# Routing products copied out of PSUM before they are scaled: one fused attention and mixture-of-adapters kernel on one core

## The chip, the cores and the metric

The kernel runs on one core of one Trainium2 chip. A core has five engines that work side by side, each through its own list of instructions in order: TensorE (PE) for matrix products, VectorE (DVE), ScalarE (ACT) and GpSimd (POOL) for elementwise work, and SyncE (SP), which here only issues transfers. Matrix products land in PSUM, eight banks of 512 fp32 columns on 128 partitions; everything else works in SBUF. The metric is the device time of one execution in microseconds; the time before is 117.84 us, the median of three runs (117.83 to 118.19).

## The reference

Linear attention with cosine weights, and then a mixture of low-rank adapters on its output. Eight batches, eight heads, 576 positions, 64 numbers a head; eight adapters of rank 16, of which each token uses two. The last lines are given in words.

```python
def phi(x, c, s):
    r = np.maximum(x, 0.0)
    return np.concatenate([r * c, r * s], axis=-1)
q_p = phi(q, cos_w, sin_w)
k_p = phi(k, cos_w, sin_w)
kv = np.einsum('bhsf,bhsd->bhfd', k_p, v)
z = np.sum(k_p, axis=2)
num = np.einsum('bhsf,bhfd->bhsd', q_p, kv)
den = np.einsum('bhsf,bhf->bhs', q_p, z)[..., None] + 1e-06
x = num / den                      # as (4608, 512)
...
logits = x @ w_gate                # 8 adapters, the best two are kept
w = softmax over the two
out = x + sum over the two of w[e] * (x @ A[e]) @ B[e]
```

Inputs are 28.85 MB of fp32 (q, k, v of 9.44 MB each and the weights), the output 9.44 MB.

## The kernel before

The work is cut into small named steps, and their order is written out by hand in one string, ORDER. A token of it such as `nd26@2` or `ex24=V` names a step, after `=` the engine that does it (V is DVE, S is ACT, G is POOL), and after `@` the buffer slots that it takes, most often PSUM banks 0 to 7. `replay` walks through the string and emits step by step; each engine gets its instructions in this order, and the framework adds the waits that the data and the buffers need. Nothing is decided on the chip: an engine whose next step isn't ready waits, and what is queued behind it waits too.

The steps, in the order in which the data goes through them:

- `LK`, `LQ`, `LV`: loads of a batch (or of two: K4, K6, Q4 and Q6 hold batches 4 and 5, or 6 and 7). All go through SP's queue. A load may only be issued when the slot that it fills is free: V7 takes V4's slot (`V_AT`), Q6 the slots of Q0 and Q3.
- `cK`, `cQ`: conversion of a third of a load to bf16; `phiK`, `phiQ`: multiplication of one of nine slices by the tangent; `vs`: multiplication of one of nine slices of V by the cosine (`vs4` does V4 and V5, `vs6` V6 and V7).
- `kv`: products of K and V on PE, `ke`: their copy out of PSUM.
- `tq`: transpose of a tile of Q on PE, `eq`: its copy out of PSUM. There are 36 tiles of 128 tokens; tiles 18 to 26 belong to batches 4 and 5, tiles 27 to 35 to batches 6 and 7.
- `nd`: numerator and denominator on PE; `rd`: reciprocal of the denominator, `nx`: the division, both DVE. `nx26` stands for tiles 26 and 27.
- `tx`, `ex`: transpose of the quotient and its copy.
- `za`: the product with the adapters A and the gate, 136 columns a tile, for a group of up to three tiles in one bank. A group is named by its last tile: 20, 23, 26, 29, 32, then 34 (two tiles) and 35 (one).
- the routing of a group, small steps all: `mx` (the two best), `nt` (their sum), `ge` (which adapters are kept), `d`, `sg` (a sigmoid on ACT), `w` (the weights), `zg` (the 128 adapter columns of each tile times the weights). `ge`, `d` and `zg` read the products from the bank that `za` wrote, which is free only after `zg`.
- `tz`, `ez`: transpose of the scaled products and its copy; `dx`: the quotient plus the product with B on PE, 512 columns; `eo`: the copy to an output buffer; `st`: the store of a group.

`fill` steps are products that nobody reads; they keep PE busy early on. The steps around the last loads stand so in ORDER before:

```
vs4.0=G@1,2 ... vs4.6=G ... LV7@1 ... st8.0 ...
st11.0 tq25 phiQ6.1=G ex20=S@1 mx19 dx15@2 vs6.0=S@0,1 vs6.8=V vs6.4=G dx16 tq26@0 eq24=V@1
...
tz20@7 phiQ6.6=G zg23 ke6=S@1 tq30@0 tz23@6 ... nd26@2 ... nx26@6 dx19 tq31 eo18=S@5 eq30=V@0 nd28@2
```

and at the end

```
za35@4 eo30=S@4 w34=G dx32@6 mx35@1 zg34 nt35=V tz34@7 eo32=S ge35 ez34=V@2 d35 dx33@2 st32.0
sg35 dx34 w35=G zg35 eo33=S@2 tz35@0 ez35=V@0 dx35@6 st34.0 eo35=S@0 st35.0
```

The functions that the change touches:

Of the kernel before, what the change touches and what calls it, by code (L numbers as in the profile page):

```python
# [18 lines left out]
NJ = 9  # L19
# [79 lines left out]
w11=G phiQ4.2=G cQ4.2=S@2 kv5.1 phiQ4.4=V kv5.2 phiQ4.1=V mx14 tx16@2 phiQ4.5=V nt14=G tq18@4
zg11 ke5=S@0 phiQ4.8=G tx17 tq19 ge14 d14 ex16=S@0 phiQ4.3=V za15@6 eq18=V@0 sg14 za16 w14=G  # L100
za17 cK6.1=S@2 tz11@3 mx15@0 tq20@4 mx16 mx17 ez11=V@2 tq21 ge17 nd18@0 cK6.2=V@0 eq20=S@1
phiK6.3=G zg14 nd19 phiK6.8=G nt17=V d17 tz14@7 rd18@2 sg17 tq22@4 phiK6.5=G ez14=S@0 nx18@1
tq23 cK6.0=S@4 phiQ4.6=G dx11@7 w17=V dx9@2 eq22=V@0 dx10 phiK6.0=G tx18@0 eo9=S@3 tx19
phiK6.4=V dx12@4 phiK6.7=G ex18=V@0 dx13 eo11=S cQ6.0=G@4 zg17 nd20@0 eo12=S@4 nd21 tz17@6
rd20@0 za18@7 nx20@0 ez17=S@1 tq24@4 phiQ6.2=G phiK6.2=S dx14@6 cQ6.1=G@0 phiQ4.7=S nd22@0
eo14=V nd23 mx18@0 tx20@6 st14.0 rd22@0 phiQ6.0=G tx21 phiQ6.3=S nx22@4 za19 st11.0 tq25
phiQ6.1=G ex20=S@1 mx19 dx15@2 vs6.0=S@0,1 vs6.8=V vs6.4=G dx16 tq26@0 eq24=V@1 eo15=S@5 tq27
vs6.5=G dx17@6 eq26=V@0 vs6.7=G nd24@2 eo17=S nd25 vs6.6=G phiK6.1=S za20 st17.0 rd24@0 tx22@6
mx20 tq28@0 vs6.2=G vs6.1=S nx24@3 st5.0 tq29 nt20=G vs6.3=S tx23 st2.0 cQ6.2=G@2 d20 kv6.0@2
ge20 sg20 ex22=V@0 phiQ6.4=S kv7.0@4 w20=V za21@6 phiK6.6=G eq28=S@1 zg20 za22 za23 mx21@1  # L110
kv7.1 mx22 mx23 ge23 kv7.2 nt23=G d23 kv6.1 ke7=V@3 sg23 kv6.2 w23=G tz20@7 phiQ6.6=G zg23
ke6=S@1 tq30@0 tz23@6 phiQ6.5=G ez20=S@2 nd26@2 ez23=V@0 nd27 phiQ6.8=V phiQ6.7=G dx18@6 rd26@0
nx26@6 dx19 tq31 eo18=S@5 eq30=V@0 nd28@2 nd29 dx21@6 rd28@2 nx28@5 tx24@0 dx22 tx25 eo21=S@2
tx26@1 tx27 ex24=V@0 nd30@2 nd31 dx20@0 rd30@1 nx30@2 tq32@6 eo20=S tq33 ex26=S@1 dx23@0
eq32=V@1 za24@3 tx28@2 za25 eo23=S tx29 za26 mx24@2 ex28=S@0 nd32@4 st23.0 mx25 mx26 ge26 nd33
nt26=V st20.0 d26 tq34@1 rd32@2 sg26 nx32@7 za27@0 w26=G eq34=S@0 tx30@2 za28 tx31 za29 mx27@1
tx32@5 ex30=S@0 mx28 tx33 mx29 zg26 nd34@6 nt29=G ge29 ex32=S@1 tz26@4 rd34@0 tq35@1 d29 nx34@0
za30@3 za31 sg29 ez26=V@0 za32 eq35=S@0 w29=G tx34@5 mx30@2 dx24@6 zg29 dx25 ex34=S@0 mx31 mx32
tz29@4 nt32=V nd35@0 ge32 eo24=S@2 d32 ez29=V@1 dx26@5 rd35@0 za33@2 nx35@1 sg32 dx27@6 eo26=S
w32=G dx28 zg32 st26.0 za34 eo27=S@1 mx33@0 tz32@4 mx34 dx29@3 ez32=V@2 nt34=G tx35@5 d34  # L120
dx30@0 eo29=V ex35=S@0 dx31 ge34 sg34 st29.0 za35@4 eo30=S@4 w34=G dx32@6 mx35@1 zg34 nt35=V
tz34@7 eo32=S ge35 ez34=V@2 d35 dx33@2 st32.0 sg35 dx34 w35=G zg35 eo33=S@2 tz35@0 ez35=V@0
dx35@6 st34.0 eo35=S@0 st35.0
# [67 lines left out]
def a_ps(n):  # L191
    return 0.16 + n / 1200.0
# [14 lines left out]
def kernel(  # L207
# [68 lines left out]
    W0, L0 = {}, {}  # L276
# [17 lines left out]
    R_zt, R_o, R_rd, R_sm = Res("zt", NZT), Res("o", NO + 3), Res("rd", 3), Res("sm", 3)  # L294
    R_ps = Res("ps", 8)
# [51 lines left out]
    o_half = add("half", {"DVE": 0.1}, [], e_half, alloc=[al(L0, "o", R_o, 3, cnt=3, only=NO)])  # L347
# [37 lines left out]
    def load(dst, src, bs):  # L385
        ap = src[bs[0]:bs[0] + len(bs)].rearrange(
            "b (g hp) (p j) d -> (hp p) (b g) (j d)", hp=2, j=NJ)
        nc.sync.dma_start(out=dst, in_=ap)  # L388
# [9 lines left out]
    for l in LOADS:  # L398
        nm, b = l[0], int(l[1])
        G = {}  # L400
        if nm == "V":
            lds[l] = (G, add("L" + l, {"SP": 0.7}, [],
                             lambda e, G=G, b=b: load(v_t[:, H2 * G["s"].slot:H2 * (G["s"].slot + 1)], v, [b]),
                             alloc=[al(G, "s", R_v, NJ, only=V_AT[b])], dma=BYT))
        else:
            units, tl, src, res = (K_UNITS, k_t, k, R_k) if nm == "K" else (Q_UNITS, q_t, q, R_q)
            bs = next(us for us in units if us[0] == b)
            nb = len(bs)
            lds[l] = (G, add("L" + l, {"SP": 0.7}, [],
                             lambda e, G=G, bs=bs, nb=nb, tl=tl, src=src:  # L410
                             load(half(tl, G["s"].slot, nb), src, bs),
                             alloc=[al(G, "s", res, 3, cnt=nb, align=nb,
                                       only=K_AT[b] if nm == "K" else None)],
                             dma=BYT * nb))
# [4 lines left out]
    def add_phi(nm, u, bs):  # L419
# [4 lines left out]
        G, ld = lds[nm + str(b)]  # L424
        for c in range(3):
# [277 lines left out]
    for bt in split(EX_TAIL):  # L703
# [22 lines left out]
        for ti in bt:  # L726
            X[ti]["ex"] = ex

    for ids in groups:
        n = len(ids)  # L730
        Gd = {}
        zas, mxs = [], []
# [167 lines left out]
```

## Time and profile before

| | |
|---|---|
| median of three runs | 117.84 us (117.83 to 118.19) |
| profiled execution, its own time | 118.06 us |
| span of its instructions | 116.3 us |
| mean granted TensorE clock | 0.976 |
| busy: PE, DVE, ACT, POOL | 98.2, 86.1, 84.1, 62.6 us |
| read and written by transfers | 28.85 and 9.44 MB |

The page of the profile gives the busy time of each engine, then the span in 40 equal slices, one digit a slice (9 is 90% or more). The chain of waits starts from the last instruction and goes back to what released each step. In a group's row stand line, engine, operation, tiles written and read, and shapes; then the count, the total busy time and the mean of one in nanoseconds, and the idle time of the engine just before. In a row of the timeline the first number is the start, the second the length, both in microseconds. "issue" is time in which an engine waited for nothing that the profile shows.

### The profile page before, as it was taken

The numbers are of one execution on the slowest core, as the hardware profiler recorded it, in microseconds if no ns is written. First come the engines' busy times: TensorE is split into PE (matmuls) and PEld (weight loads), VectorE is DVE, ScalarE is ACT, GpSimd is POOL, SyncE is SP. The second block draws the span as 40 slices with busy tenths as digits, with TensorE's granted clock in tenths as the row PEclk, the third lists the DMA queues.
The fourth block names the chain that finished last, engine by engine and source line by source line (L and its number), as shares of the span: only waits on it lengthen the run. The fifth ranks groups of instructions, "written<-read, shape, count | busy, mean of one in ns | idle before, by whom it ended". The sixth has DMA issues, their size and how long they took to land.

```text
span 116.3 us, 4552 instructions
## 1 busy us (share of the span) xinstructions
PE 98.2 (84%) x1954; PEld 73.5 (63%) x1954; DVE 86.1 (74%) x211; ACT 84.1 (72%) x126; POOL 62.6 (54%) x119
## 2 busy tenths in 40 slices
PE   5999988679595959999987869999999699999830
PEld 1344465469494948686866766785897588976200
DVE  1157766394789989999899888797998788887510
ACT  7305568394998887997959798987993349897850
POOL 3074678259169699649978346995967000101100
PEclk9999999985999999999999999999999999999996
DMA  2999999999999999999999999999996001923994
GB/s 42 388 401 391 393 391 392 393 305 390 392 392 387 392 391 393 387 391 392 392 394 385 393 391 391 388 413 406 386 406 264 23 0 46 414 92 129 378 403 172
DMA packets 15827, 38.57 MB, mean 332 GB/s; under 512 B 1728, under 2 KB 1728, under 8 KB 15808
## 3 DMA queue, kind: packets, MB, share of 16 engines
q1 hardware_dynamic: 15808, 38.29, 87.8%
q8 instruction: 15, 0.25, 0.9%
q14 instruction: 4, 0.03, 0.1%
HBM read 28.85 MB, written 9.44 MB: 329 GB/s over the span
## 4 chain that ended last, share of the span: by engine, by line
PE 36%; DMA 29%; DVE 14%; ACT 8%; SPq 4%; issue 4%; POOL 1%; POOLq 0%; DVEq 0%; ACTq 0%
DMA q<-in_q_dram 14%; DMA v<-in_v_dram 14%; PE psum L604 8%; DVE x L692 6%; PE psum L837 6%; PE psum L738 5%; PE psum L713 5%; SPq L388 4%; PE psum L654 4%; PE psum L500 4%; DVE qt L623 3%; ACT o L302 2%; PE psum L647 2%; ACT qt L621 2%; PE psum L799 1%
## 5 line engine op out<-in xcount | busy, mean ns | idle before, releaser
L604 PE MATMUL psum<-ident,qp 128*128 128x128 bf16 x288 | 21.5, 226 | 1.9 <-DVE qp L313 1.8
L692 DVE TENSOR_TENSOR x<-psum,rd 128x1024 bf16<-128x1024 f32 (+1 forms) x19 | 22.2, 1168 | 1.1 <-PE psum L864 0.6
L313 POOL TENSOR_SCALAR kp<-kp,tanw 128x256 bf16<-128x256 bf16 (+1 forms) x29 | 16.7, 587 | 10.0 <-ACT kp L440 10.0
L604 PEld LDWEIGHTS <-qp 128*128 128x128 bf16 x288 | 18.2, 102 | 3.1 <-DVE qp L313 1.9
L313 POOL TENSOR_SCALAR vb<-v,cosw 128x256 bf16<-128x256 f32 (+1 forms) x30 | 17.6, 604 | 3.1 <-DMA v<-in_v_dram 3.1
L440 ACT ACTIVATE kp<-k 128x768 bf16<-128x768 f32 (+1 forms) x12 | 12.5, 1054 | 7.5 <-DMA k<-in_k_dram 7.1
L864 PE MATMUL psum<-ident 128*128 128x512 bf16 (+1 forms) x70 | 16.4, 388 | 1.4 <-POOL ident masks.py:199 1.4
L623 DVE TENSOR_SCALAR qt<-psum 128x2048 bf16<-128x2048 bf16 x12 | 14.5, 1219 | 1.3 <-PE psum L604 1.2
L713 PE MATMUL psum<-ident,x 128*128 128x128 bf16 x144 | 12.5, 221 | 3.0 <-DVE x L692 2.8
L304 POOL CAST qp<-q 128x768 bf16<-128x768 f32 (+1 forms) x10 | 11.2, 1128 | 6.3 <-DMA q<-in_q_dram 6.3
L302 ACT COPY o<-psum 128x1024 f32<-128x1024 f32 (+1 forms) x12 | 9.9, 840 | 6.4 <-PE psum L837 6.2
L837 PE MATMUL psum<-x,ident 128*64 128x512 bf16 (+1 forms) x48 | 13.9, 385 | 0.6 <-DVE x L692 0.6
L837 PE MATMUL psum<-Bb,zt 128*64 128x512 bf16 (+1 forms) x48 | 13.8, 379 | 0.3 <-DVE zt L306 0.2
L713 PEld LDWEIGHTS <-x 128*128 128x128 bf16 x144 | 9.8, 114 | 6.1 <-DVE x L692 2.5
L738 PE MATMUL psum<-AW,xt 128*128 128x136 bf16 x144 | 12.7, 223 | 0.9 <-ACT xt L302 0.4
L621 ACT ACTIVATE qt<-psum 128x2048 bf16<-128x2048 bf16 (+1 forms) x7 | 11.4, 1628 | 2.2 <-PE psum L604 2.1
L313 POOL TENSOR_SCALAR qp<-qp,tanw 128x256 bf16<-128x256 bf16 (+1 forms) x20 | 11.5, 583 | 2.7 <-DVE qp L306 2.5
L500 PE MATMUL psum<-vb,kp 64*128 64x65 bf16 x576 | 11.7, 190 | 1.4 <-issue 0.6
L864 PEld LDWEIGHTS <-ident 128*128 128x128 bf16 x70 | 7.0, 104 | 9.1 <-issue 2.4
L780 POOL TENSOR_TENSOR w<-ge,ex 128x24 f32<-128x24 f32 (+2 forms) x10 | 2.3, 231 | 18.8 <-ACT ex L776 18.7
L500 PEld LDWEIGHTS <-kp 64*128 64x128 bf16 x576 | 9.9, 94 | 3.2 <-issue 1.5
L654 PE MATMUL psum<-kv,qt 128*64 128x65 bf16 x384 | 9.8, 197 | 2.1 <-issue 1.6
(60 smaller groups left out, 172.7 us busy)
## 6 DMA issues: line engine op xcount, KB each, us to landing
v<-in_v_dram SPq DMA_DIRECT2D x8, 1152.0 KB, 16.0
q<-in_q_dram SPq DMA_DIRECT2D x4, 1152.0 KB, 15.0
k<-in_k_dram SPq DMA_DIRECT2D x4, 1152.0 KB, 10.0
k<-in_k_dram SPq DMA_DIRECT2D x2, 2304.0 KB, 19.9
q<-in_q_dram SPq DMA_DIRECT2D x2, 2304.0 KB, 19.8
out_dram<-o SPq DMA_DIRECT2D x6, 768.0 KB, 5.5
out_dram<-k SPq DMA_DIRECT2D x5, 768.0 KB, 5.7
out_dram<-o SPq DMA_DIRECT2D x1, 512.0 KB, 2.7
```

Of the source, the lines that this page charges most:

```text
L313: eng.tensor_scalar(out=o_ap, in0=i_ap, scalar1=by, scalar2=0.0, op0=ALU.mult, op1=ALU.add)
L440: nc.scalar.activation(o_ap, i_ap, AF.Relu)
L500: nc.tensor.matmul(out=psum[:, s + hp, h2 * W:(h2 + 1) * W], lhsT=kp[hp * 64:hp * 64 + 64, bi * H2 + h2, :], rhs=vb_t[hp * 64:hp * 64 + 64 ...
L604: nc.tensor.transpose(out=o_ap[:, h2, :, hi, :], in_=qv[:, bi * H2 + h2, :], identity=ident)
L621: nc.scalar.activation(o_ap, i_ap, AF.Relu)
L623: nc.vector.tensor_scalar(out=o_ap, in0=i_ap, scalar1=0.0, scalar2=None, op0=ALU.max)
L654: nc.tensor.matmul(out=psum[hi * 64:hi * 64 + 64, s + g, x * W:(x + 1) * W], lhsT=qt[:, qi, h2, hp, hi, :], rhs=kv_t[KV[b]["kv"].slot][:, ...
L692: nc.vector.tensor_tensor(out=x_t[Y["x"].slot][:, 0:n].rearrange("p n (g i d) -> p (n g) i d", g=2, i=4), in0=f()[:, :, :, 0:D], in1=r().t ...
L713: nc.tensor.transpose(out=bank16(s, 1024)[:, i * 512 + c * 128:i * 512 + (c + 1) * 128], in_=xv[:, c, :], identity=ident)
L738: nc.tensor.matmul(out=psum[:, s, i * ZW:(i + 1) * ZW], lhsT=xt_t[Z["xt"].slot][:, zi, c, :], rhs=AW[:, c, :], start=(c == 0 and i == 0), ...
L837: nc.tensor.matmul(out=o, lhsT=w, rhs=r, start=not last, stop=bool(last), skip_group_check=True)
L864: nc.tensor.matmul(out=psum[:, s % 8, c:], lhsT=ident, rhs=warm[:, c:], start=s < 8, stop=True, skip_group_check=True)
```

## The change

Three things are changed. First, for the groups 18-20, 21-23, 24-26, 27-29 and 30-32 (`ZS_GROUPS`), which hold the tiles of batches 4 to 7 but for the last three, a new step `zc` copies the products of `za` (408 fp32 columns) from PSUM to an SBUF buffer `zs`; the bank is free when `zc` and the three `mx` are done. `ge`, `d` and `zg` then read the copy, and `zg` may run on POOL. The buffers `zs` lie in `k_t[1]`, the tile that K6 is the last to fill, and can be used once K6 is converted. Second, of the last four stores the two that hold three tiles are split into one of two tiles and one of one tile (`ST_SPLIT`); each part waits only for its own copy. Third, ORDER is another: all five `zc` are on ACT, `zg20`, `zg26` and `zg29` on POOL, `zg23` and `zg32` on DVE; the last loads come as V7, V6, Q6 instead of Q6, V6, V7; and the groups 34 and 35 are routed side by side.

```diff
+ST_SPLIT = 4
+ZS_GROUPS = (6, 7, 8, 9, 10)
...
+    ZS_LAST, NZS = 5, 4
+    zs_t = [k_t[1].rearrange("p g x -> p (g x)")[:, 3 * ZW * i:3 * ZW * (i + 1)].rearrange(
+        "p (n z) -> p n z", z=ZW) for i in range(NZS)]
...
-                     alloc=[al(Gd, "za", R_ps, 1)] if i == 0 else [],
+                     alloc=[al(Gd, "za", R_ps, 1 + n * zcopy)] if i == 0 else [],
...
+            if zcopy:
+                return zs_t[Gd["zs"].slot][:, 0:n]
             return psum[:, Gd["za"].slot, 0:n * ZW].rearrange("p (n z) -> p n z", z=ZW)
...
+            def e_zc(e, Gd=Gd, n=n):
+                copy(e, zs_t[Gd["zs"].slot][:, 0:n].rearrange("p n z -> p (n z)"),
+                     psum[:, Gd["za"].slot, 0:n * ZW])
+            zcs = [add(f"zc{ids[-1]}", {"ACT": a_ps(n * ZW), "DVE": d_ps32(n * ZW)}, zas[-1:], e_zc,
+                       alloc=[al(Gd, "zs", R_zs, 1)], free=[(Gd, "za")])]
...
-            nc.vector.tensor_tensor(
+            eng = nc.vector if e == "DVE" else nc.gpsimd
+            eng.tensor_tensor(
                 out=sm("zg"),
...
-        o_ge = add(f"ge{ids[-1]}", {"DVE": 0.175}, [mxs[-1]], e_ge)
-        o_d = add(f"d{ids[-1]}", {"DVE": 0.18}, [o_nt], e_d)
+        o_ge = add(f"ge{ids[-1]}", {"DVE": 0.175}, [mxs[-1]] + zcs, e_ge)
+        o_d = add(f"d{ids[-1]}", {"DVE": 0.18}, [o_nt] + zcs, e_d)
...
+        cuts = [(0, 2), (2, 3)] if n == 3 and gi >= len(outs) - ST_SPLIT else [(0, n)]
+        for y, (i0, i1) in enumerate(cuts):
+            def e_st(e, i0=i0, i1=i1, rows=rows, Gd=Gd):
+                nc.sync.dma_start(out=rows[:, i0:i1], in_=o_t[Gd["o"].slot][:, i0:i1, :])
```

The loading code is rewritten so that a load could be cut in parts, but each load stays one transfer. Of the new ORDER, the places that the prediction speaks of:

```
vs4.0=G@1,2 ... vs4.2=S ... vs4.7=G vs4.1=S ... vs4.4=G ... vs4.6=G vs4.8=S ... vs4.3=G vs4.5=S ... LV7@1 ... LV6@0 ... LQ6@2 ... st8.0
...
zc20=S@0 eq24=V@1 tx23 dx15@6 cQ6.2=S@0 cQ6.0=G@4 za21@4 dx16 mx20 mx21@1 nd24@0 ex22=V@0 nd25
eo15=S@4 phiQ6.2=G ge20 dx17@5 phiQ6.1=V vs6.3=G za22 rd24@0 eo17=S tq26@6 nx24@2 za23 phiQ6.0=G
vs6.4=S st17.0 st2.0 zc23=S@1 vs6.5=V tq28@0 phiK6.4=S nt20=V kv7.0@2 mx22 mx23 ge23 tq27 nt23=G
d23 d20 tq29 sg23 vs6.7=V sg20 w23=G kv7.1 eq26=V@0 eq28=S@1 w20=G kv7.2 zg20=G kv6.0@4 kv6.1
zg23=V cQ6.1=G@2 kv6.2 ke7=V@2 tz23@6 ke6=S@0 tz20@7 ez23=V@2 nd26@0 ez20=S@1 phiQ6.8=V nd27
phiQ6.5=G phiQ6.3=S dx21@4 rd26@2 phiQ6.4=G nx26@5 dx22 tq30@6 eo21=S@5 tq31 dx18@0 eq30=V@0
phiQ6.6=S dx19 nd28@2
...
zc26=S@2 ... eq35=S@0 ... zc29=S@0 ... ex32=S@1 ... zc32=S@3 ... ex35=S@0
...
za35@2 eo27=S@3 za34 mx35@1 tz32@7 dx29@6 nt35=V ez32=V@2 d35 eo29=S dx30@0 st29.0 mx34 ge35 dx31
nt34=V sg35 d34 st29.1 ge34 dx32@4 sg34 w35=V eo30=S@5 w34=G zg35 zg34 tz35@2 ez35=V@1 tz34@5
eo32=S dx35@6 st32.0 ez34=V@0 dx33@0 st32.1 eo35=V@1 dx34 st35.0 eo33=S@4 st34.0
```

More of the change, by code (lines that the diff above doesn't have):

```diff
@@ L103 @@
[L103 to L114, printed above, removed]
@@ new lines @@
+tq26@6 nx24@2 za23 phiQ6.0=G vs6.4=S st17.0 st2.0 zc23=S@1 vs6.5=V tq28@0 phiK6.4=S nt20=V
+kv7.0@2 mx22 mx23 ge23 tq27 nt23=G d23 d20 tq29 sg23 vs6.7=V sg20 w23=G kv7.1 eq26=V@0 eq28=S@1
+w20=G kv7.2 zg20=G kv6.0@4 kv6.1 zg23=V cQ6.1=G@2 kv6.2 ke7=V@2 tz23@6 ke6=S@0 tz20@7 ez23=V@2
+nd26@0 ez20=S@1 phiQ6.8=V nd27 phiQ6.5=G phiQ6.3=S dx21@4 rd26@2 phiQ6.4=G nx26@5 dx22 tq30@6
+eo21=S@5 tq31 dx18@0 eq30=V@0 phiQ6.6=S dx19 nd28@2 eo18=S@2 nd29 tq32@6 rd28@2 nx28@6 tx24@0
+tx25 tq33 tx26@1 eq32=S@1 tx27 ex24=V@1 nd30@2 nd31 ex26=V@0 dx20@0 rd30@2 za24@1 nx30@7 za25
@@ L124 @@
+zg32=V za35@2 eo27=S@3 za34 mx35@1 tz32@7 dx29@6 nt35=V ez32=V@2 d35 eo29=S dx30@0 st29.0 mx34
+ge35 dx31 nt34=V sg35 d34 st29.1 ge34 dx32@4 sg34 w35=V eo30=S@5 w34=G zg35 zg34 tz35@2
+ez35=V@1 tz34@5 eo32=S dx35@6 st32.0 ez34=V@0 dx33@0 st32.1 eo35=V@1 dx34 st35.0 eo33=S@4
+st34.0
 """
@@ L727 @@
             X[ti]["ex"] = ex
-    for ids in groups:
+    for gi, ids in enumerate(groups):
         n = len(ids)
```

156 lines of the change are left out of this document (87 added, 69 removed).

## The prediction

> **What bounds the kernel now.** I read the slices of the page first, then the busy time by stage, the chain of waits in order of time, and last the timeline at the places the chain named.
>
> ```profile
> DMA  2999999999999999999999999999996001923994
> GB/s 42 388 401 391 393 391 392 393 305 390 392 392 387 392 391 393 387 391 392 392 394 385 393 391 391 388 413 406 386 406 264 23 0 46 414 92 129 378 403 172
> ```
>
> A slice is 116.3 / 40 = 2.91 us. The transfers run at about 390 GB/s without a gap until slice 30, fall to nothing near 93 us, and come back for the stores. So there are two stages: up to about 80 us the loads set the pace, and after that something else does.
>
> ```profile
> 70.00:80.00 10.00, 9.66 (x179) 7.03 (x173) 8.03 (x15) 8.16 (x13) 7.60 (x10) 1.00 1.04 399
> 80.00:90.00 10.00, 9.79 (x303) 8.40 (x302) 9.23 (x22) 7.66 (x12) 8.33 (x13) 1.00 0.90 363
> 90.00:100.00 10.00, 8.97 (x210) 7.62 (x208) 8.49 (x16) 5.81 (x8) 0.24 (x1) 1.00 0.17 66
> 100.00:110.00 10.00, 9.60 (x129) 6.36 (x127) 7.79 (x33) 8.83 (x14) 1.09 (x5) 1.00 0.57 230
> 110.00:116.30 6.30, 1.55 (x6) 0.31 (x4) 0.52 (x2) 1.81 (x3) 0.21 (x1) 0.83 0.75 297
> ```
>
> The columns after the stage's length are PE, PE's weight loads, DVE, ACT and POOL, then granted clock, DMA share and GB/s. From 80 to 110 us PE and DVE are both nearly full, ACT has room except in the last ten, POOL does almost nothing after 90, and the clock is full. The chain shows which of them hands on:
>
> ```profile
> 63.30 16.49 DMA v<-in_v_dram
> ...
> 87.74 0.45 PE psum L604 x8
> ...
> 89.63 1.24 DVE x L692
> ...
> 90.90 0.32 PE psum L654 x8
> 91.22 0.62 issue
> ...
> 105.49 0.86 PE psum L837 x4
> ...
> 106.63 0.26 DVE m L749 x2
> ...
> 111.42 0.40 PE psum L837
> 111.85 0.59 ACT o L302
> ```
>
> The last load, V7, lands at 63.30 + 16.49 = 79.79. One DVE result (nx26) holds the chain until 90.86, PE carries it to 106.6, then comes the routing of the last two groups, and the last copy ends at 111.85 + 0.59 = 112.44. What follows to 116.3, 3.86 us, is the last store and the end of the program.
>
> ```profile
> 79.88 0.73 ACT L310 ACTIVATE vb<-v,cosw 128x512 bf16<-128x512 f32 x1 [0.72 <-DMA v<-in_v_dram]
> 79.89 0.49 DVE L313 TENSOR_SCALAR vb<-v,cosw 128x512 bf16<-128x512 f32 x1 [0.78 <-DMA v<-in_v_dram]
> 79.95 0.99 POOL L313 TENSOR_SCALAR vb<-v,cosw 128x512 bf16<-128x512 f32 x1 [1.23 <-DMA v<-in_v_dram]
> ```
>
> Three engines stood idle for 0.7 to 1.2 us until that load came: there is no backlog at 79.9 us. The kernel is therefore 79.9 us of loading, about which the change can do little, and 36.4 us of tail, where everything has to be won or lost.
>
> **The change, part by part.** *The loads.* The same bytes are loaded; the last three become V7, V6, Q6 in place of Q6, V6, V7. V7 goes into V4's slot, so its issue must wait for the nine vs4 steps, and V6 and Q6 now queue behind that wait on SP. In the kernel before:
>
> ```profile
> 55.05 4.07 POOL L313 TENSOR_SCALAR vb<-v,cosw 128x512 bf16<-128x512 f32 x6 [0.28 <-DMA v<-in_v_dram]
> 57.41 8.65 SPq L388 DMA_DIRECT2D v<-in_v_dram  x2
> ```
>
> V4 and V5 are in by 55.05. The new order gives five vs4 steps to POOL (5 x 0.68 = 3.4) and four to ACT, so V7 can be issued at about 59. What is already queued then (up to K6) lasts until the three last loads have their turn: 4.72 MB at 0.392 MB/us is 12.0 us, 79.8 - 12.0 = 67.8. Less the 2 or 3 us of a transfer's way, there are about 6 us of cover. I cost this at nothing; without cover each us of lateness would be a us of the result. The rearranged work up to 80 us likewise hides behind the transfers, which the slices show saturated. So the last load again lands at 79.9.
>
> *From the load to tile 28's products (nd28).* The rows for this part:
>
> ```profile
> L623 DVE TENSOR_SCALAR qt<-psum 128x2048 bf16<-128x2048 bf16 x12 | 14.5, 1219 | 1.3 <-PE psum L604 1.2
> L783 DVE TENSOR_TENSOR zg<-psum,w 128x384 bf16<-128x384 f32 x11 | 6.0, 549 | 0.1
> L313 DVE TENSOR_SCALAR qp<-qp,tanw 128x512 bf16<-128x512 bf16 x5 | 2.1, 440 | 0.0
> L313 DVE TENSOR_SCALAR vb<-v,cosw 128x512 bf16<-128x512 f32 x2 | 1.0, 479 | 0.8 <-DMA v<-in_v_dram 0.8
> L304 POOL CAST qp<-q 128x1536 bf16<-128x1536 f32 x4 | 5.9, 1463 | 0.3 <-DMA q<-in_q_dram 0.3
> L313 POOL TENSOR_SCALAR qp<-qp,tanw 128x512 bf16<-128x512 bf16 x9 | 6.2, 695 | 0.2
> L780 POOL TENSOR_TENSOR w<-ge,ex 128x24 f32<-128x24 f32 x8 | 1.9, 236 | 15.9 <-ACT ex L776 15.8
> L780 POOL TENSOR_TENSOR w<-ge,ex 128x8 f32<-128x8 f32 x1 | 0.2, 206 | 1.8 <-ACT ex L776 1.8
> L776 ACT ACTIVATE ex<-d 128x24 f32<-128x24 f32 x11 | 2.4, 222 | 0.4 <-DVE d L766 0.3
> 84.77 0.48 DVE L780 TENSOR_TENSOR w<-ge,ex 128x24 f32<-128x24 f32 x1
> 86.77 0.70 DVE L306 CAST kv<-psum 128x520 bf16<-128x520 f32 x1
> 90.77 1.22 DVE L623 TENSOR_SCALAR qt<-psum 128x2048 bf16<-128x2048 bf16 x1
> ```
>
> On DVE, before, 79.89 to 90.86 is 10.97 us from the load to the end of nx26. In the new order this stretch loses eq24 (1.22, now ahead of the load), vs6.8 (0.48), w20 (0.48) and zg20 (0.55), the last two to POOL; it gains phiQ6.1 (0.44), vs6.5 and vs6.7 (0.96) and nt20 (estimated at 0.2, from POOL's small forms): -2.73 + 1.60 = -1.1. phiQ6.1 must wait for POOL's cast cQ6.0, 1.46 after the load, where DVE would come to it at 1.2: +0.3. So nx26 ends at 90.86 - 0.8 = 90.1, and eq30, which began at 90.77, can begin at 90.1.
>
> eq30 also needs tq31, and that hangs on POOL, since Q6 now lands last: cQ6.0, phiQ6.2, vs6.3, phiQ6.0, then nt23, w23, w20 and **zg20**, then cQ6.1, phiQ6.5, phiQ6.4. w20 can't start before d20 on DVE and two sg steps on ACT (2 x 0.22). Behind d20 come vs6.7 and eq26 (0.48 + 1.22) and the steps from ke7 to nx26, 90.86 - 86.77 = 4.1 before, with 0.5 of idle in it: 90.1 - 1.7 - 3.6 = 84.8 at the latest, so w20 starts at 85.3. Until there POOL's first four steps (1.46 + 3 x 0.7 = 3.6, to 83.5) have 1.8 us to spare. From there it goes step by step: 0.24 + zg20 + 1.46 + 2 x 0.695, and 0.45 for tq31. No row has zg on POOL. From below: a one-input step of 512 elements takes 0.695, so some 0.6 for 384. From the same operation: 206 ns for 8 elements and 236 for 24 are 1.9 ns an element, 0.206 + 376 x 0.0019 = 0.92. From above: twice that, 1.8, if DVE gets in its way (the two w's quoted show what a collision does: DVE's took 480 ns beside a busy POOL). I take 0.92, the nearest row; tq31 then ends at 89.8, just in time.
>
> [...]
>
> *The second thing the copy does* is turn ge, d and zg of groups 20 to 32 into DVE operations that read both operands from SBUF, where they read one from PSUM.
>
> ```profile
> L780 DVE TENSOR_TENSOR w<-ge,ex 128x24 f32<-128x24 f32 x3 | 1.0, 338 | 0.0
> L771 DVE TENSOR_TENSOR ge<-psum,m 128x24 f32<-128x24 f32 x11 | 1.9, 175 | 0.1
> ```
>
> w and ge have the same 24 elements; the one with both operands in SBUF takes 338 against 175. If ge23, d23 and d20 go that way, 3 x 0.16 = 0.5, and zg23 may double (0.55): at most +1.0 in this stretch, at least 0. POOL is busy in part of it only; I take +0.3. With -0.8 from above the stretch gives **-0.5**.
>
> *From nd28 to the routing of the last groups.* PE has dx21 and dx22 behind it here, which stood behind nd28 before: 2 x 0.43 = 0.86 less for PE (0.86 for x4 is the row at 105.49). But before, DVE and ACT handed to PE as often as PE held them up, and DVE's list is the same length, so I count half, **-0.4**. The copies zc26, zc29 and zc32 stand on ACT ahead of eq35, ex32 and ex35:
>
> ```profile
> L302 ACT COPY o<-psum 128x512 f32<-128x512 f32 x5 | 3.0, 593 | 0.0
> L302 ACT COPY k<-psum 128x1024 f32<-128x1024 f32 x5 | 5.0, 1009 | 2.4 <-PE psum L837 2.2
> L306 DVE COPY o<-psum 128x512 f32<-128x512 f32 x2 | 1.4, 686 | 0.1
> ```
>
> 408 columns are, between these forms (0.81 ns a column), 0.51 each, 1.5 together. ACT gives eo26 and eo35 to DVE and gets ez26 and eo29, about even; it had 4.2 us free from 90 to 100, so the copies go in there at no cost. If that room is gone, they cost up to 1.5. The banks come free at once in exchange, a few us earlier; what that is worth the trace does not show: from 0 to the 1.4 us that PE is idle between 90 and 110 (1.03 + 0.40). I count none in the forecast.
>
> *The end.* Groups (33,34) and (35) are now routed side by side, and the last copy is eo33 (1.01) in place of eo35 (0.59): +0.4. Before, the small steps of the two groups ran one after another, 106.63 to 111.42 in the chain; side by side they save at least one w and its hand-over, an estimated 0.4 from the w row of 0.21: -0.4. The splits only put 2 more issues on SP, which is idle; they bring st32's bytes forward by half a us.
>
> ```profile
> out_dram<-o SPq DMA_DIRECT2D x1, 512.0 KB, 2.7
> out_dram<-o SPq DMA_DIRECT2D x1, 256.0 KB, 2.7
> ```
>
> The last store becomes the 512 KB one, which took as long as the 256 KB one: **0**.
>
> The sum is -0.5 - 0.4 = -0.9 us. The profiled execution took 118.06 (116.3 of span and 1.76 around it), 0.22 above the median of 117.84; 118.06 - 0.9 = 117.2, on the median's scale **117.0 us**.
>
> **The rivals.** *POOL is late (slower).* Everything after 90 us waits for tq31, and POOL reaches it with nothing to spare. The mechanism is that POOL and DVE hinder each other in this stretch. If zg20 takes 1.8 instead of 0.92, and the three larger steps behind it run as the first one after the load did (0.99 at 79.95, against 0.68 for its like at 55.05: 0.3 more each), tq31 comes 0.9 + 0.9 = 1.8 late; less the 0.9 gained that is +0.9, 117.84 + 0.9 = 118.7. With zg20 alone at its upper price it only cancels the gain; it makes the kernel slower from about 1.25 us of lateness on. For it: POOL was the busiest stage of its run here (8.33 of 10), and Q's way from load to use is longer than V's. Against it: at 55 us six steps in a row ran at their usual length. [...]
>
> *No change.* ACT has no room after 100 us (8.83 of 10). If the copies zc29 and zc32 (1.0 us) push ex32 and ex35 back, they eat the gain: 117.0 + 0.9 = 117.9 or a little under it.
>
> *More gain.* If it was the banks that kept PE from running through (in 90 to 100 it was busy 8.97), and they no longer do, PE's missing 1.0 us there comes on top: 116.0.
>
> **How the numbers follow.** The forecast (116.4 to 117.4) has 0.45, more gain 0.10, no change 0.20, late POOL 0.25. What a measurement can tell from no change is 0.3%, 0.35 us. A quarter of the no-change case lies below 117.49, so faster has 0.45 + 0.10 + 0.05 = 0.60, same 0.15, slower 0.25. The range runs from 115.8, just below the case of more gain, to 118.9, just above the late POOL; what it leaves out is a late POOL whose d20 is late as well (DVE's upper price, 0.35 more) and some of the far gain, under 0.2. The forecast's own range is 116.4 to 117.4.
>
> **What would show it.** Right: the last load (now Q6) still lands within 0.5 us of 79.8; zg on POOL near 0.9; eq30 begins near 90.1 to 90.4; PE's idle after 90 no larger than now; about 3.9 us from the last copy's end to the end of the span. Wrong, and slower: PE waiting for phi steps of POOL around 88 to 90 us, ge and d near 340 ns, or V7 landing with a gap in the GB/s slices 22 to 26.

## The result, and the profile after

The kernel after takes 116.72 us (median of 4 runs, 116.69 to 116.83) against 117.89 us for the kernel before beside it (4 runs, 117.83 to 118.19). The ratio is 0.9897, with a 95% interval of 0.9879 to 0.9916: 1.2 us faster. The ratios leave slow executions out, such as one of the kernel with two copies that took 120.33 us at a mean granted clock of 0.967, where the median is 117.83. The profiled execution took 116.70, its span 114.9.

Line numbers are 8 to 36 higher than before (in the experiments mostly one less): `tq` is L621, `eq` on DVE L640, `nd` L671, `nx` L709, `zg` L813, `dx` L869, the store L889; `zc` is the ACT row L310 with 408 columns, its buffer appears as `k`. First the slices of the page:

```profile
DMA  2999999999999999999999999999895004972995
GB/s 38 405 397 393 391 393 390 396 305 389 391 390 392 394 382 391 389 390 392 391 392 387 396 386 391 391 401 422 340 376 211 6 0 167 381 288 103 401 392 200
```

The loads run without a gap as before. Then the busy time by stage (length, PE, weight loads, DVE, ACT, POOL, clock, DMA share, GB/s):

```profile
80.00:90.00 10.00, 8.30 (x250) 6.96 (x249) 7.89 (x18) 8.72 (x13) 8.16 (x11) 1.00 0.70 284
90.00:100.00 10.00, 10.00 (x234) 8.53 (x233) 8.79 (x20) 7.95 (x11) 2.13 (x5) 1.00 0.36 139
100.00:110.00 10.00, 9.03 (x108) 5.39 (x108) 7.45 (x31) 7.91 (x16) 1.73 (x5) 1.00 0.71 284
110.00:114.90 4.90, 0.00 (x0) 0.00 (x0) 0.00 (x0) 0.68 (x1) 0.00 (x0) 0.81 0.70 273
```

From 90 to 100 us PE has no gap at all (8.97 before), and after 110 it does nothing (1.55 before). The timeline at the places that the prediction named, and the groups:

```profile
59.91 2.93 SPq L399 DMA_DIRECT2D q<-in_q_dram  x1
79.86 1.47 ACT L310 CAST qp<-q 128x1536 bf16<-128x1536 f32 x1 [1.77 <-DMA q<-in_q_dram]
...
85.53 0.84 POOL L813 TENSOR_TENSOR zg<-k,w 128x384 bf16<-128x384 f32 x1
86.32 1.79 POOL L312 CAST qp<-q 128x1536 bf16<-128x1536 f32 x1
88.85 1.22 DVE L709 TENSOR_TENSOR x<-psum,rd 128x1024 bf16<-128x1024 f32 x1
90.42 1.23 DVE L640 TENSOR_SCALAR qt<-psum 128x2048 bf16<-128x2048 bf16 x1 [0.35 <-PE psum L621]
91.10 0.45 PE L671 MATMUL psum<-kv,qt 128*64 128x65 bf16 x16
...
109.67 1.01 ACT L310 COPY k<-psum 128x1024 f32<-128x1024 f32 x1 [0.73 <-PE psum L869]
110.71 0.33 SPq L889 DMA_DIRECT2D out_dram<-k  x1
```

```profile
L813 POOL TENSOR_TENSOR zg<-k,w 128x384 bf16<-128x384 f32 x3 | 2.5, 839 | 0.2
L310 ACT COPY k<-psum 128x408 f32<-128x408 f32 x5 | 2.5, 497 | 0.8 <-DVE m L767 0.5 <-PE psum L621 0.2
L800 DVE TENSOR_TENSOR ge<-k,m 128x24 f32<-128x24 f32 x5 | 1.2, 236 | 0.0
L795 DVE SCALAR_TENSOR_TENSOR d<-k,ss 128x24 f32<-128x24 f32 x5 | 0.8, 166 | 0.1
L809 POOL TENSOR_TENSOR w<-ge,ex 128x24 f32<-128x24 f32 x8 | 3.5, 442 | 4.4 <-ACT ex L805 4.4
```

The mean of 442 ns for w misleads: the median (the middle number of the next line, least and greatest beside it) is 237, as before. Two of the w, at 49.14 and 66.66 us, took 974 and 1031 ns; the first copy stands at 77.60, so they have nothing to do with the change.

```profile
L809 POOL TENSOR_TENSOR w<-ge,ex x9: 221/237/1031, 36.3 to 107.3; 128x24 f32<-128x24 f32 x8, 128x16 f32<-128x16 f32 x1
```

The last load, now Q6, lands at 79.8 as V7 did. Against before, the places along the way stand so:

| | before, us | after, us | |
|---|---|---|---|
| nx26 ends (DVE) | 90.86 | 90.07 | -0.8 |
| eq30 begins (DVE) | 90.77 | 90.42 | -0.35 |
| nd28 begins (PE) | 90.90 | 91.10 | +0.2 |
| nd29 ends (PE) | 92.5 | 91.9 | -0.6 |
| nd32 begins (PE) | 98.06 | 96.59 | -1.5 |
| dx24 begins (PE) | 103.11 | 101.76 | -1.35 |
| last copy ends (ACT) | 112.44 | 110.68 | -1.8 |
| end of the span | 116.3 | 114.9 | -1.4 |

nd28 begins a little later than before, with dx21 and dx22 done ahead of it, and without the stop of 0.62 us that PE made in the middle of it ("91.22 0.62 issue" in the prediction's chain). From 85.34 to 102.9 us PE runs through. From the last copy to the end of the span it is now 4.2 us (3.86 before).

Part of what the new order does is done before the last load lands: nd24 and nd25, which stood at 81.57 before, now start at 79.14 (first line before, second after), and from 80 us on, by the rows of the stages, PE has 592 matmuls left where it had 648.

```profile
81.57 0.44 PE L654 MATMUL psum<-kv,qt 128*64 128x65 bf16 x16
79.14 0.44 PE L671 MATMUL psum<-kv,qt 128*64 128x65 bf16 x16
```

### The profile page after: what moved, and what is told of

Its sections match the earlier page's. It is cut to its first block, busy times and chain, and to the rows that moved or that the text cites. A ratio compares the mean times of both kernels' runs of the same rounds, so it can differ in the third digit from the quotient of the medians.

```text
span 114.9 us, 4548 instructions
## 1 busy us (share of the span) xinstructions
PE 97.1 (85%) x1953; PEld 71.1 (62%) x1953; DVE 85.2 (74%) x207; ACT 84.6 (74%) x130; POOL 67.6 (59%) x124
## 4 chain that ended last, share of the span: by engine, by line
PE 55%; DVE 18%; DMA 17%; POOL 2%; issue 2%; ACT 2%; SPq 0%; POOLq 0%; DVEq 0%
DMA q<-in_q_dram 17%; PE psum L900 14%; PE psum L621 9%; PE psum L869 8%; DVE x L709 7%; PE psum L517 7%; PE psum L730 6%; PE psum L756 6%; DVE qt L640 5%; PE psum L671 3%; PE psum L664 2%; ACT k L310 1%; POOL qp L312 1%; PE psum L831 1%; DVE rd L704 1%
## 5 line engine op out<-in xcount | busy, mean ns | idle before, releaser
L709 DVE TENSOR_TENSOR x<-psum,rd 128x1024 bf16<-128x1024 f32 (+1 forms) x19 | 22.2, 1166 | 1.2 <-PE psum L900 0.7
L621 PE MATMUL psum<-ident,qp 128*128 128x128 bf16 x288 | 19.9, 219 | 1.9 <-ACT k L310 1.6
L900 PE MATMUL psum<-ident 128*128 128x512 bf16 (+1 forms) x69 | 17.8, 411 | 2.5 <-POOL ident masks.py:199 1.8
L621 PEld LDWEIGHTS <-qp 128*128 128x128 bf16 x288 | 17.0, 98 | 4.3 <-issue 3.0
L321 POOL TENSOR_SCALAR qp<-qp,tanw 128x256 bf16<-128x256 bf16 (+1 forms) x31 | 17.7, 578 | 1.9 <-ACT qp L310 1.4
L640 DVE TENSOR_SCALAR qt<-psum 128x2048 bf16<-128x2048 bf16 x11 | 13.3, 1219 | 2.0 <-PE psum L621 2.0
L638 ACT ACTIVATE qt<-psum 128x2048 bf16<-128x2048 bf16 (+1 forms) x8 | 13.2, 1654 | 1.9 <-PE psum L621 1.9
L321 POOL TENSOR_SCALAR vb<-v,cosw 128x256 bf16<-128x256 f32 (+1 forms) x24 | 13.7, 585 | 1.4 <-DMA v<-in_v_dram 1.4
L310 ACT COPY k<-psum 128x1024 f32<-128x1024 f32 (+2 forms) x17 | 12.3, 736 | 2.9 <-PE psum L869 2.1
L869 PE MATMUL psum<-x,ident 128*64 128x512 bf16 (+1 forms) x48 | 13.9, 385 | 0.4 <-DVE x L709 0.4
L869 PE MATMUL psum<-Bb,zt 128*64 128x512 bf16 (+1 forms) x48 | 13.8, 379 | 0.0
L756 PEld LDWEIGHTS <-xt 128*128 128x128 bf16 x144 | 9.6, 98 | 2.9 <-issue 0.6
L314 DVE COPY xt<-psum 128x1024 bf16<-128x1024 bf16 x15 | 10.1, 681 | 0.7 <-PE psum L730 0.6
```

The costliest lines, as they stand in the source:

```text
L310: nc.scalar.copy(o_ap, i_ap)
L321: eng.tensor_scalar(out=o_ap, in0=i_ap, scalar1=by, scalar2=0.0, op0=ALU.mult, op1=ALU.add)
L621: nc.tensor.transpose(out=o_ap[:, h2, :, hi, :], in_=qv[:, bi * H2 + h2, :], identity=ident)
L638: nc.scalar.activation(o_ap, i_ap, AF.Relu)
L640: nc.vector.tensor_scalar(out=o_ap, in0=i_ap, scalar1=0.0, scalar2=None, op0=ALU.max)
L709: nc.vector.tensor_tensor(out=x_t[Y["x"].slot][:, 0:n].rearrange("p n (g i d) -> p (n g) i d", g=2, i=4), in0=f()[:, :, :, 0:D], in1=r().t ...
```

## The experiments

Three theories on where the 1.2 us came from: banks that come free earlier (A in the expectations), VectorE relieved by GpSimd (B), and the order of steps (C). Two more came out of the traces: the end is bound by the stores, and PE waits for its own instructions. Times are ratios to the kernel before in the same series of runs, with 95% intervals; after is 0.9897.

**zg back on VectorE.** In the kernel after:

```diff
-zg20=G ... zg26=G ... zg29=G
+zg20=V ... zg26=V ... zg29=V
```

> The changed kernel with the three multiplications zg20, zg26 and zg29 back on DVE; the copies stay. Theory A (banks: the gain comes from PE always having a product ready, because the copies free banks that the new order uses): 116.6 to 116.9, no change to speak of, and PE still without a gap from 90 to 100 us. Theory B (DVE's load: the gain comes from taking 3 x 0.55 = 1.65 us off DVE): DVE ends later by up to that, 117.2 to 117.9. A third outcome, faster than 116.6, would mean that POOL's 0.84 against DVE's 0.55 delays tz20, tz26 and tz29.

117.39 us, 0.9946 (0.9934 to 0.9958): half of the gain is gone. The timeline:

```profile
86.11 1.53 DVE L812 TENSOR_TENSOR zg<-k,w 128x384 bf16<-128x384 f32 x2
...
87.70 0.51 PE L830 MATMUL psum<-ident,zg 128*128 128x128 bf16 x6 [0.54 <-DVE zg L812]
89.34 1.23 DVE L708 TENSOR_TENSOR x<-psum,rd 128x1024 bf16<-128x1024 f32 x1
90.91 1.23 DVE L639 TENSOR_SCALAR qt<-psum 128x2048 bf16<-128x2048 bf16 x1 [0.34 <-PE psum L620]
```

DVE now does both zg one after the other, PE waits 0.54 us for the second, and nx26, eq30 and the last copy all come 0.5 to 0.6 us later. Behind that PE still runs through (10.00 of 10 from 90 to 100), so this half of the gain is DVE's load.

**Fewer copies.** In the kernel after, one copy (and in a second kernel two, `(6, 7)`); the other groups are scaled out of PSUM on DVE, and a few steps take another bank:

```diff
-ZS_GROUPS = (6, 7, 8, 9, 10)
+ZS_GROUPS = (6,)
-zc23=S@1 ... kv6.0@4 ... zc26=S@2 ... zg26=G ... zc29=S@0 ... za30@1 ... zg29=G zc32=S@3 ... tz29@0 ... dx27@0
+kv6.0@0 ... zg26=V ... za30@0 ... zg29=V ... tz29@1 ... dx27@4
```

No run has the new order without any copy: while group 20's products stay in their bank, the two neighbouring banks that nd24 needs are not free.

> The changed kernel with only the copy zc20; groups 23, 26, 29 and 32 are scaled straight from PSUM on DVE, and kv6.0, za30, tz29 and dx27 take other banks, since the old ones are no longer free. Theory A (banks): PE waits for banks again, kv6 above all, which now needs the banks of tq28: 117.2 to 118.0. Theory C (the order of the steps alone is what gains; the copies are a cost on ACT): four copies of 0.50 us less on ACT, so 116.3 to 116.7. Theory B (DVE's load): zg26 and zg29 on DVE again, 117.0 to 117.5, and the same as the run with zg on DVE within 0.3.

> The kernel after with copies for groups 20 and 23 alone (out of five); groups 26, 29 and 32 are scaled from PSUM by VectorE, and their banks are held until then. With one copy the time was 119.32, with all five and the scaling on VectorE 117.39. In the run with one copy PE waited 1.13 us for a bank at 87.26 and 0.87 us for another at 101.04. The second copy gives back the bank of the first wait, not that of the second: 118.2 to 118.4 by banks. If it is VectorE's load that counts, the same 119.3 as with one copy, less the 0.1 that one zg from SBUF saves. If only the first two copies count, 117.4.

One copy: 119.32 us, 1.0110 (1.0096 to 1.0124). Two: 117.83 us, 0.9991 (0.9959 to 1.0024), against 0.9946 for five with zg on DVE. In the timeline with one copy PE waits twice for a bank:

```profile
87.26 1.27 PE L516 MATMUL psum<-vb,kp 64*128 64x65 bf16 x72 [1.13 <-ACT qt L637]
101.04 0.87 PE L755 MATMUL psum<-AW,xt 128*128 128x136 bf16 x12 [0.87 <-DVE zg L812]
```

kv6 waits for the bank that eq28 empties, and za30 for zg29's. With the second copy the first wait is gone and the second is still there (0.87 at 101.07). By the ratios the first wait is worth about 1.4 us (0.0119 of 118), the second and the rest about 0.5. So the copies don't speed anything up by themselves: they are what lets PE follow the new order without waiting for banks.

**The copies in the old order.** The kernel before with the copies alone, each right behind its group's last `za`, zg on DVE, stores unsplit:

```diff
-za20 ... za23 ... za26 ... za29 ... za32
+za20 zc20=S@0 ... za23 zc23=S@1 ... za26 zc26=S@2 ... za29 zc29=S@3 ... za32 zc32=S@0
```

> The kernel before in its own order, with the five copies put in (on ACT, right behind the last za of each group) and nothing else: zg stays on DVE, stores unsplit. The banks come free earlier but the order does not use it. Theory A: the copies bring nothing by themselves and cost ACT time, 117.9 to 118.6. Theory B predicts the same or a little slower. If freeing a bank early helps by itself, through waits that the framework then does not need, 117.3 to 117.7.

120.81 us, 1.0231 (1.0217 to 1.0246): 2.8 us slower than before, and worse than either theory said. The timeline, ACT, DVE and PE:

```profile
85.85 1.86 ACT L637 ACTIVATE qt<-psum 128x2048 bf16<-128x2048 bf16 x1
87.61 0.49 ACT L309 COPY k<-psum 128x408 f32<-128x408 f32 x1
...
88.13 0.32 DVE L766 MAX8 m<-psum 128x8 f32<-128x8 f32 x3 [1.68 <-ACT k L309]
91.64 1.23 DVE L708 TENSOR_TENSOR x<-psum,rd 128x1024 bf16<-128x1024 f32 x1
...
90.17 0.34 PE L830 MATMUL psum<-ident,zg 128*128 128x128 bf16 x3 [1.19 <-DVE zg L812]
```

The copy of group 23 stands behind a 1.86 us step on ACT; DVE's list stands still for 1.68 us until it is done, nx26 with it (91.64 against 89.63 before), and PE for 1.19. It is already `mx`, which reads the same bank as the copy, that starts only when the copy has ended (88.13, the copy 87.61 + 0.49 = 88.10). Here a copy of 0.49 us went with a wait of 1.68 on DVE, over three times its length. In the new order zc23 stands ahead of that step (eq28). Of the 2.8 us, 2.0 are there by nx26; where the rest arises is open.

**The splits.** Taken back in after, and put alone into before (the same edit the other way round):

```diff
-ST_SPLIT = 4
+ST_SPLIT = 0
-st29.0 ... st29.1 ... st32.0 ... st32.1
+st29.0 ... st32.0
```

> The changed kernel without the split of the stores of groups 29 and 32. If the split matters, st32's bytes go out up to 0.6 us later and push the last store st34 back: 116.9 to 117.3. If st34 waits only for its own copy eo33, nothing changes: 116.7 within 0.1. All theories on the middle stretch say the same here.

> The kernel before with one part of the change alone: the stores of groups 29 and 32 (768 KB each) cut in two, 512 KB and 256 KB. Taking the split back from the kernel after cost 0.4 to 0.5 us. If the split is worth as much in the kernel before, 117.4 to 117.5 against 117.9; but before has its last store 2.6 us behind the one ahead of it (issues at 109.84 and 112.46) and a smaller one, so the queue has more time to run empty: 117.6 to 117.9 if that counts. Nothing: 117.9.

Without the split after takes 117.21 us, 0.9948 (0.9922 to 0.9974): 0.5 to 0.6 us more, though the last copy ends only 0.07 later. In before it does nothing: 118.03 us, 1.0003 (0.9989 to 1.0017). The stages of 2 us show why (clock, DMA share, GB/s). After:

```profile
104.00:106.00 2.00, 1.00 0.24 98
106.00:108.00 2.00, 1.00 1.01 408
108.00:110.00 2.00, 1.00 1.01 399
110.00:112.00 2.00, 1.00 0.99 379
112.00:114.00 2.00, 0.77 0.73 289
```

Without the split:

```profile
106.00:108.00 2.00, 1.00 0.85 341
108.00:110.00 2.00, 1.00 0.97 393
```

Before:

```profile
106.00:108.00 2.00, 1.00 0.68 280
108.00:110.00 2.00, 1.00 0.89 359
110.00:112.00 2.00, 1.00 1.03 418
```

In after the transfers are full from 106 us to the last byte at 113.6, at 379 to 408 GB/s. The end is set less by the last copy than by these 2.95 MB of stores, and 0.13 MB not moved from 106 to 108 is 0.33 us at the end. In before the transfers have room until 110, so what the split brings forward there would be mostly waited out again; that is argued, not shown. (The 2.6 us that the second expectation has between the last two stores are 0.63: st34 is issued at 111.83, between 109.84 and 112.46.)

**The last two groups.** In after, one after the other as in before:

```diff
-mx35@1 ... nt35=V ... d35 ... nt34=V ... zg35 zg34 ... eo35=V@1 dx34 st35.0 eo33=S@4 st34.0
+nt34=V ... zg34 nt35=V tz34@5 ... dx34 w35=G zg35 eo33=S@4 ... dx35@6 st34.0 eo35=S@1 st35.0
```

and, the other way, the products of groups 33 and 34 copied at the same time on ACT and DVE, the last store cut in halves:

```diff
-dx34 st35.0 eo33=S@4 st34.0
+dx34@1 st35.0 eo33=S@4 eo34=V st34.0 st34.1
```

> The kernel after, with the routing of the last two groups one after the other as the kernel before has it (group 34, then group 35; out of the copies the last is that of group 35 on ScalarE, and the last store is its 256 KB); all else as after. If side by side is worth the 0.4 us of the prediction, the last copy ends 0.4 us later (111.1 in place of 110.68); if the 0.8 us that the two traces suggest, 0.8 us later (111.5). The smaller last store gives 0.3 us back (it ended 3.84 us after its issue before, 4.17 us after). So 116.8 by the prediction's term, 117.2 by the reading of the traces; 116.7 or less if the order at the end does nothing.

> The kernel after, with the products of groups 33 and 34 copied out separately (33 on ScalarE, 34 on VectorE, at the same time, instead of both by one ScalarE copy of 1.01 us), and the last store cut in two stores of 256 KB. If the end is the copy and then the bytes of the last store, the copy ends 0.3 to 0.4 us earlier (110.3 in place of 110.68) and the end comes 3.85 us behind the last issue instead of 4.17: 115.9 to 116.4. If only the copy counts, 116.4; if the stores before it fill the queue anyway, 116.7.

One after the other: 117.25 us, 0.9922 (0.9903 to 0.9940), 0.3 us more by the ratios, with intervals that overlap. The last copy ends at 111.71, 1.0 us later than in after (0.3 of it is there at 103 us already, before the routing), but the span is only 0.5 longer. Halves: 117.14 us, 0.9914 (0.9895 to 0.9932): no gain, nearest to the last of the three cases expected. Both fit an end set by the stores: when after's last store is issued (110.71), 0.5 MB of others are still ahead of it, 1.3 us of transfer. A last copy that came 1.0 us later cost half of that or less, and halving the last copy and the last store bought nothing.

Taken back one by one, zg on POOL, the splits and the order at the end cost 0.6, 0.6 and 0.3 us, more than the 1.2 gained. They don't add up, and the gain can't be shared out among them.

**PE's stops.** The trace of before has three places where PE stops in the middle of a step with nothing to wait for (0.65, 0.94 and 0.62 us), one of them in the chain. To see whether they go by the place in PE's list, the fills ahead of everything are recut, half the width and twice the number for the same PE time, in before (first pair) and in after (three variants):

```diff
-fill=50@0
+fill=2@0 fill=96@8
...
-fill=53@0
+fill=3@0 fill=100@8
+fill=49@0 fill=8@8
+fill=25@0 fill=56@8
```

Each fill more is a matmul and a weight load more in front of the rest. The pieces of 16 KB and 256 instructions that the last two expectations speak of are read from the traces; the counts stand behind the table of stops.

> The kernel before, with 48 more and shorter fills ahead of its first load (50 fills of full width become 2 of full width and 96 of half), so that PE is busy there for about the same time and every later matmul stands some 48 matmuls further in PE's list. The trace of before has stops in the middle of a step on PE, put down to issue: 0.65 at 63.33, 0.94 at 69.53, 0.62 at 91.84, the last one inside the chain. If these hang on the place in PE's list, they move, and the time becomes 117.2 to 117.5 if the last one leaves the chain: then some 0.6 us of the gain of the change is where such a stop fell, and not the order. If they hang on what PE waits for, they stay with nd28 and the time is within 0.2 us of 117.9. Third: it is all the chain's, and the time is unchanged though the stops move.

> The same for the kernel after: 50 of its 53 fills become 100 of half the width, so that every later matmul stands 50 matmuls further in PE's list. Its trace has one such stop (0.56 at 62.19), none where PE sets the time. If stops go by the place in PE's list, one may fall between 84 and 110, where PE has no gap, and the time becomes 117.2 to 117.4; else within 0.2 us of 116.72.

> The kernel after with 4 of its first 53 fills made into 8 of half the width: every later matmul stands 4 matmuls and 4 weight loads further in PE's list, and the 16 KB pieces in which that list is fetched (256 instructions each) end 8 instructions earlier in the program. Counted in the trace of after, the end of a piece then still falls where PE has 5 us for the piece before it, so no stop is added: within 0.2 us of after's 116.72 (116.5 to 116.9). If more instructions cost time by their number, as 100 cost 2.5 us, 8 would cost 0.2: 116.9.

> The same with 28 of the 53 fills made into 56: 56 PE instructions more ahead of everything. Now a piece ends in the numerators and denominators at about 88.6, some 3 us after the piece before it began to run down, and a stop of 1 to 2.6 us is expected there, on the chain: 117.7 to 119.3. If the cost goes by the number of instructions, 56 cost 1.4 us (118.1) and no stop is seen there. If neither, 116.7.

| kernel | PE instructions added | time, us | ratio to before |
|---|---|---|---|
| before | 96 | 122.47 | 1.0332 (1.0284 to 1.0380) |
| after | 8 | 116.87 | 0.9894 (0.9875 to 0.9912) |
| after | 56 | 120.60 | 1.0204 (1.0181 to 1.0226) |
| after | 100 | 119.36 | 1.0100 (1.0076 to 1.0124) |

The times are medians of the executions that the ratio takes. Neither of the first two took the time expected: in before no stop left the chain, a longer one came into it; in after one fell between 84 and 110, but of 2.15 us. With 56 more the time is above the range expected, and the stop that was to come at 88.6 came at 93.85. Nor does the cost go by the number: 56 cost more than 100, and 8 cost nothing, as expected. The waits of PE, before with 96 and after with 100 more:

```profile
PE psum L653 <- issue: 2.9, 1, 2.9
```

```profile
PE psum L670 <- issue: 2.4, 2, 2.2
```

The trace also lists each transfer, and the "q8 instruction: 15" of the page are 15 transfers of 16 KB. Set against them, each stop ends shortly behind one, and always at the same place of PE's list, counted in matmuls and weight loads in the order of their starts:

| kernel | stop, us | 16 KB transfer, us | first PE instruction behind the stop |
|---|---|---|---|
| before | 91.22 to 91.84 | 89.46 to 90.42 | 3263 = 12 x 256 + 191 |
| before | 62.69 to 63.33 | 60.83 to 61.87 | 1983 = 7 x 256 + 191 |
| before, 96 more | 89.36 to 92.28 | 90.00 to 90.96 | 3260 = 12 x 256 + 188 |
| after | 61.63 to 62.19 | 59.69 to 60.74 | 1983 = 7 x 256 + 191 |
| after, 100 more | 88.34 to 90.49 | 88.29 to 89.21 | 3259 = 12 x 256 + 187 |
| after, 56 more | 93.85 to 94.91 | 92.73 to 93.69 | 3263 = 12 x 256 + 191 |

In the traces of all fourteen kernels PE stops 26 times for 0.2 us or more with "issue" as the only cause. All 26 lie 187 to 191 past a multiple of 256 (a few matmul records can be missing, which moves the count), and all end 1.2 to 1.6 us after the end of a 16 KB transfer. The numbers fit too: the page of after has 1953 matmuls and 1953 weight loads, 3906 PE instructions for 15 transfers, 260 to each. From this I infer that PE's list comes in pieces of 256, and that a piece that is used up before the next one is there costs a stop; this is read from places, times and counts, as no counter shows it. The 256 instructions ahead of a stop had run in 2.6 to 6.3 us: in 2.6 and 3.3 ahead of the stops of 2.15 and 2.93, in 5.3 ahead of those of 0.2 to 0.3. With 56 more, a first stop of 1.21 us comes at 41 us, and the granted clock of that stage is 0.69, against 1.00 in after, while the loads still run:

```profile
40.00:50.00 10.00, 7.04 (x69) 4.57 (x66) 5.75 (x12) 5.72 (x8) 5.44 (x12) 0.69 1.05 389
```

The work then falls behind the loads, V7 and V6 are issued at 61.90 in place of 58.14, and the rest of the kernel is late by that. This is read from an execution of 122.84 us, longer than those in the table; their mean granted clock, 0.973 to 0.975 against 0.991 to 0.998 in after, makes a fall in them likely, but doesn't show where it was. With 100 more, in an execution of 120.92 us, the clock falls too, to 0.50, behind the stop that ends at 90.49 (stages of 2 us). Two of the three executions in the table have a mean clock of 0.996, so their longer time does not need this fall:

```profile
88.00:90.00 2.00, 0.34 (x20) 0.25 (x16) 0.47 (x2) 1.12 (x3) 1.68 (x3) 1.00 0.10 36
90.00:92.00 2.00, 1.35 (x24) 0.91 (x26) 0.88 (x2) 0.00 (x0) 0.00 (x0) 0.91 0.03 8
92.00:94.00 2.00, 2.00 (x18) 1.75 (x17) 0.69 (x2) 1.63 (x2) 0.00 (x0) 0.50 0.00 0
94.00:96.00 2.00, 2.00 (x44) 1.01 (x42) 1.14 (x1) 0.61 (x1) 0.00 (x0) 0.73 0.00 0
```

In before with 96 more, a longer stop, 2.93 us to 92.28, left the clock at 1.00:

```profile
90.00:92.00 2.00, 0.00 (x0) 0.00 (x0) 0.14 (x1) 0.00 (x0) 0.00 (x0) 1.00 0.06 18
92.00:94.00 2.00, 1.66 (x36) 1.23 (x38) 0.97 (x2) 0.06 (x1) 0.00 (x0) 1.00 0.04 8
```

So the clock fell to 0.50 behind a stop of 2.15 us and stayed at 1.00 behind one of 2.93. The length of a stop alone does not decide it, and that the stops bring the clock down is not shown.

## Why the prediction was right, and where it was mis-sized

*The loads, 0.* Right: the last load lands at 79.79 in both, V7's issue came at 58.14 (about 59 forecast), no gap in the slices.

*From the load to nd28, -0.5.* Right as far as DVE goes: nx26 ends at 90.07 (90.1 forecast), eq30 begins at 90.42 (90.1 to 90.4), zg on POOL takes 0.84 (0.92). nd28 itself begins 0.2 later, but with the 0.86 of dx21 and dx22 done ahead of it. The +0.3 for operands in SBUF is not there: in this stretch ge takes 173 and 182 ns and d 174 and 183, not 340 (the mean of 236 comes from one ge of 470 at 97.17, beside a phi step on POOL). One larger step took longer: POOL's cQ6.1 takes 1.79 us instead of 1.46, and zg23, with both operands in SBUF, runs on DVE at 86.22 to 86.79, within it; that the one slows the other is not shown, as no run tested it by itself. So POOL was late by some 0.3 us (its last phi step ends at 89.57, by the prediction's sum at 89.3), and eq30 waited 0.35 for tq31; the late POOL of the rival needed 1.25.

*From nd28 to the routing, -0.4.* This was the term most mis-sized. I counted half of the 0.86 us of dx21 and dx22, since PE had been held up by DVE and ACT as often as it held them up. After, PE has no gap from 85.34 to 102.9, and the whole 0.86 counts: the table's step from -0.6 to -1.5, where PE has no gap before either (dx23, which also left this stretch, and tq35, which came into it, are about as long). Of the 1.03 us that PE stood still from 90 to 100 before, 0.41 was the wait for nx26 and 0.62 the stop, which I had quoted as "issue" and asked no cause for; it lies in the step from +0.2 to -0.6. By its place (3263 = 12 x 256 + 191) I put it down to PE's instruction list. In after PE makes no stop of this kind of 0.2 us or more behind the one that ends at 62.19. How much of the 1.2 us this is can't be said exactly, as no run took the stop out of before and left its order; by the table it is up to 0.6. In the new order 8 instructions more did nothing (0.9894), 56 or 100 more turned the gain into a loss (1.0204 and 1.0100).

*The copies at no cost.* Right where they stand (497 ns each, 510 forecast), but not in general: in the old order they cost 2.8 us (1.0231). *The banks, "I count none".* The question was put wrongly. Banks are no bonus on top of the order, they are what it needs: with one copy instead of five, PE waits 1.13 and 0.87 us and the kernel is 1.9 us slower than with five and zg on DVE. The rival of more gain (PE runs through) named the right mechanism; only the forecast's own -0.9 wasn't to be added to it a second time.

*The end, 0.* The sum came near by luck, through two errors. Side by side brings the last copy 0.7 to 1.0 us forward, not 0.4, so even with the longer eo33 it comes earlier. But then the end is set by the stores, and the way from the copy to the end grew by 0.4: that a 512 KB store takes as long as one of 256 KB was read from one of each and doesn't hold with 0.5 MB ahead of it. And the splits, counted at nothing, are worth 0.5 in this order.

Together the span went down by 1.4 where 0.9 was forecast; the result lies inside the forecast's own range because the two terms that were too small (PE without gaps, side by side) and the one that was left out (stores one behind the other) partly cancel. That the forecast of 117.0 came this near is thus partly luck. The case of no change did not come: ACT kept 4 us free from 90 to 110 with all copies in it.

## What to carry to other kernels

A buffer copy that frees a bank is worth what the order can do with the bank: judge the two together, and put the copy where no in-order engine has to wait for it (here the five copies cost 2.8 us in the old order, with a wait of 1.68 us on DVE, and were part of a gain of 1.2 in the new one). Where the last stores run into each other, look at GB/s in steps of 2 us before shortening the last copy: here 2.95 MB at 379 to 408 GB/s set the end more than that copy, and without the split the kernel took 0.5 us longer though the copy ended only 0.07 later. And an idle time in the middle of a PE step that nothing explains is worth counting in PE instructions: here 56 and 100 instructions more ahead of everything else cost 3.6 and 2.4 us and 8 cost nothing, and the stops lay 187 to 191 past a multiple of 256.

## What the runs showed of the hardware that I had not expected

- The trace of after has 15 transfers of 16 KB, 0.88 to 1.23 us each, for 3906 PE instructions. PE's 26 stops of 0.2 to 2.9 us in the fourteen traces all lie 187 to 191 past a multiple of 256 and end 1.2 to 1.6 us after the end of such a transfer; pieces of 256 are what I infer from that. From 47 to 78 us in after, with the loads running, the transfers follow one another every 6.2 to 6.4 us, 41 PE instructions a us; that this is a limit was not tested.
- In after the two-input operation zg of 128x384 fp32 took 839 ns on GpSimd (three of them), against 554 on VectorE from the same buffers (two). The small ones (128x24) took 237 in the median, but the one at 66.66 us took 1031, beside a conversion of K on VectorE that ran from 66.64 for 0.96 us.
- From 106 us to the last byte at 113.6 the stores of after move 2.95 MB, at 379 to 408 GB/s in the full stages; that late output takes 7.6 us.
